# Moving one output store in the last batch and casting W1 in eighths in the first, in a fused attention and MLP kernel

## The chip, the cores and the metric

The kernel runs on one core of a Trainium2 chip. The metric is the time of one execution in microseconds (us) on the device. Profiles give times from the first instruction of the program; the span of a profile is some 1.8 us shorter than the time of the same execution.

## The reference, cut to what matters

```python
# u, v: 8 x 3008 x 256, z: 8 x 3008 x 64, all float32
scores = (1 / S) * z @ z.transpose(0, 2, 1)
out = u * ((np.maximum(scores, 0) ** 2) @ v)          # per batch
x = out.reshape(24064, 256)
h = x @ w_in                                          # 256 x 2048
g = h / (1 + np.exp(-1.702 * h))
return g @ w_out                                      # 2048 x 256
```

## The kernel before

The eight batches follow one another. A batch has six query chunks of 512 rows (`i` = 0 to 5; "the fourth chunk" is `i` = 3). Each chunk runs through attention steps `n` (its slots); at fixed slots other work is put in: scores for a later chunk (`take`), loads, turns. The last chunk or the one before it is also interleaved with the up projection, in groups of 256 hidden columns (`up_group`); the down projection follows. Scores are symmetric, so blocks of the attention matrix are reused, transposed by DMA (`tt`, `ad`, `al`, all issued by SyncE, in order).

```python
def cast_w(k):                 # ScalarE: a float32 quarter of W1 to float16
    act.activation(W1[:, :, k * DFF // 4:(k + 1) * DFF // 4], WS.pop(k), AF.Copy, scale=1.0)
...
CASTW = {(3, 8): 0, (3, 40): 1, (4, 8): 2, (4, 14): 3}     # (chunk, slot): quarter, first batch only
...
elif name == "P3" and k > NCH - 3 and b < B - 1:
    LAST2.append(lambda: store(b, k))      # the last two blocks of a batch are stored in the next batch
...
if i == 3 and n in (3, 26) and LAST2:      # where they are stored
    LAST2.pop(0)()
...
if b == 0 and i == NCH - 1 and n in (8, 30, 42):
    wsums.pop(0)()                         # VectorE: sums of blocks of W2; the first needs W2's quarters 1 and 2
```

`store` makes a transposing copy on VectorE and issues four DMAs from SyncE.

Of the kernel before, what the change touches and what calls it, by code (L numbers as in the profile page):

```python
# [15 lines left out]
def kernel(  # L16
# [13 lines left out]
    AF = mybir.ActivationFunctionType  # L30
# [4 lines left out]
    DFF = moe_w_in.shape[1]  # L35
# [20 lines left out]
    dve, act, pe, sp, pool = nc.vector, nc.scalar, nc.tensor, nc.sync, nc.gpsimd  # L56

    const = ctx.enter_context(tc.tile_pool(name="const", bufs=1))
    W1 = const.tile([P, NCC, DFF], F16, name="W1")
# [17 lines left out]
    ZP, WS = {}, {}  # L77
# [43 lines left out]
    def first_cast(g, by_act=False):  # L121
        m = g % CB * CB
        for c in range(2):
            dst, src = ZT["st"][g // CB][:, m:m + CB, c, :], ZT["f"][g // CB][:, m:m + CB, :]
            if by_act:
                act.activation(dst, src, AF.Copy, scale=1.0)
            else:
                dve.tensor_copy(dst, src)

    def first_zt(g):  # L130

        z2 = ZT["st"][g // CB][:, g % CB * CB:(g % CB + 1) * CB]
        zp = ZP[g] if g in ZP else ps1.tile([P, CB, P], F16, name="zp", tag="ps1")
        for k in range(CB):
            pe.transpose(zp[:, k, :], z2[:, k, :, :], ident)  # L135

        def copies():
            zt = ZT[0][:, g * CB:(g + 1) * CB, :].rearrange("d n p -> d (n p)")
            nb = CB if g < NCH - 1 else CB - 1
            dst = zt[:, :nb * P].rearrange("d (p n) -> d p n", n=nb)  # L140
            src = zp[:, :nb, :].rearrange("d n p -> d p n")
            if g in (0, 2, 3):
                act.activation(dst, src, AF.Copy, scale=1.0)  # L143
            else:
                dve.tensor_copy(dst, src)
            if nb < CB:
                dve.tensor_copy(zt[:, nb * P:], zp[:, nb, :])

        return copies


    def load_z(b):
        ZT[b] = pz.tile([P, NJ, P], F16, name="ZT", tag="ZT")
        for n0 in range(0, NJ, NU):
            zst = pw.tile([P, NU, 2, DQK], F16, name="zst", tag="y")
            full = min(NU, NJ - 1 - n0)
            src = z[b, n0 * P:(n0 + full) * P].rearrange("(n p) d -> p n d", p=P)
            pool.dma_start(zst[:, :full, 0, :], src)
            if full < NU:
                for h in range(2):  # L160
                    pool.dma_start(zst[h * SREM:(h + 1) * SREM, full, 0, :], z[b, S0:S])
            pool.tensor_copy(zst[:, :, 1, :], zst[:, :, 0, :])
            sp.dma_start_transpose(ZT[b][:, n0:n0 + NU], zst.rearrange("p n c d -> p (n c d)"))
# [24 lines left out]
    def load_u(b, i):  # L188
        eng = pool if b else sp
        n = width(i)  # L190
        uq = pu.tile([P, CH // QW, QW, NCC], F32, name="uq", tag="uq")
        src = u[b, i * CH:i * CH + n].rearrange("(q t) c -> t q c", t=QW)
        for k in range(P // QW):
            cs = slice(k * NCC * QW, (k + 1) * NCC * QW)
            eng.dma_start(uq[k * QW:(k + 1) * QW, :n // QW].rearrange("t q c k -> t q (c k)"), src[:, :, cs])  # L195
        UQ[b, i] = uq

    def turn_u(b, i):
        n = width(i)
        ut = pu.tile([P, NCC, CH // QW, QW], F32, name="ut", tag="ut")  # L200
        UT[b, i] = ut
        dve.transpose(
            ut[:, :, :n // QW, :].rearrange("p k q t -> p q k t"),
            UQ.pop((b, i))[:, :n // QW].rearrange("p q c k -> p q k c"),
        )
# [114 lines left out]
    def full(b):  # L320

        return NCH - 2 if b < B - 1 else NCH - 1
# [116 lines left out]
    def load_w(k):  # L439

        if k < 2:
            hold = const.tile([P, 1], F16, name=f"hold{k}")
            pool.tensor_copy(hold, XT[0, k + 1][:, 0, :1])
        if k < 4:
            WS[k] = pw.tile([P, NCC, DFF // 4], F32, name="wst", tag="y")
            pool.dma_start(WS[k], moe_w_in.rearrange("(p k) f -> p k f", k=NCC)[:, :, k * DFF // 4:(k + 1) * DFF // 4])
        else:
            fs = slice((k - 4) * CB, (k - 3) * CB)
            pool.dma_start(W2[:, fs], moe_w_out.rearrange("(fo p) c -> p fo c", p=P)[:, fs])

    def cast_w(k):
        act.activation(W1[:, :, k * DFF // 4:(k + 1) * DFF // 4], WS.pop(k), AF.Copy, scale=1.0)  # L452

    def weight_sums():
        b11, b12, b21, b22 = W2K[:, LO, 0], W2K[:, LO, 1], W2K[:, HI, 0], W2K[:, HI, 1]
# [108 lines left out]
    LAST2 = []  # L564
# [67 lines left out]
    LOADW = {  # L632
        (2, 16): 0, (3, 0): 1, (3, 9): 2, (3, 41): 3, (4, 28): 4, (4, 34): 5, (4, 40): 6, (5, 0): 7,
    }
    CASTW = {(3, 8): 0, (3, 40): 1, (4, 8): 2, (4, 14): 3}
    LOAD = {(3, NJ + 20): 4, (4, NJ + 5): 5}

    FIRST_ZT, FIRST_CAST = {12: 4, 20: 5}, {5: 4, 13: 5}
# [11 lines left out]
    def take(b, n):  # L650
        for post_ in scores(b, [queue.pop(0) for _ in range(n)]):
            post_()

    def fill(b):
        assert not queue
        queue.extend(u_ for i in range(NCH) for u_ in pieces(b, i))
# [28 lines left out]
    for b in range(B):  # L685
        nup = NCH * NFG
        more = b + 1 < B
        sched = SCHED0 if b == 0 else SCHED if more else SCHED_LAST
        turn, load = (TURN, LOAD) if b else (TURN0, LOAD0)
        head = 0  # L690
        for i in range(NCH):
            host = b + 1 if more and i == NCH - 1 else b
            if host > b:
                fill(host)
                LATE.append(host)
            for n, step in enumerate(attend(b, i, b == 0 and i == 0)):
                if b == 0 and i == 0 and n in (5, 24):
                    load_u(0, n // 24)
                if b == 0 and i == 0 and n == 2:
                    copies = first_zt(3)  # L700
                if b == 0 and i == 0 and n == 3:
                    copies()
                if b == 0 and i == 0 and n in FIRST_CAST:
                    first_cast(FIRST_CAST[n], True)
                if b == 0 and i == 0 and n in FIRST_ZT:
                    first_zt(FIRST_ZT[n])()
                if (i, n) in turn:
                    turn_u(b, turn[i, n])
                if i == 3 and n in (3, 26) and LAST2:
                    LAST2.pop(0)()  # L710
                if (i, n) in load:
                    load_u(b, load[i, n])
                if b == 0 and (i, n) in CASTW:
                    cast_w(CASTW[i, n])
                if b == 0 and (i, n) in LOADW:
                    load_w(LOADW[i, n])
                if more and (i, n) == (NCH - 2, 2 if b else 16):
                    load_z(b + 1)
                if b == 0 and i == NCH - 1 and n in (8, 30, 42):
                    wsums.pop(0)()  # L720
                take(host, sched[i].get(n, 0))
                if i == full(b) and n >= HEAD and (n - HEAD) * LAGY // (2 * NJ - 10) >= head and head < LAGY:
                    up_group(b, head)
                    head += 1
                step()
        late.sort(key=lambda t: t[0])
        if more:
            for i in range(2):
                load_u(b + 1, i)
            for n0 in range(0, NJ, VB):  # L730
                load_v(b + 1, n0)
        prods = products(b)
        for q in range(head, nup):
            if more and q in (head + 14, head + 20):
                k = int(q == head + 20)
                turn_u(b + 1, k)
                load_u(b + 1, k + 2)
            up_group(b, q)
            if b == 0 and q == head + 3:
                wsums.pop(0)()  # L740
            product(b, *prods.pop(0))
            if q >= 30 and q % 2 and late:
                late.pop(0)[1]()
        steps = [lambda kp=kp: product(b, *kp) for kp in prods]
        for step in steps:
            step()
            for sum_ in [SUMS.pop(0) for _ in range(min(len(SUMS), 1 + (len(SUMS) > 4)))]:
                sum_()
            for _, turn_it in [late.pop(0) for _ in range(min(len(late), 1 + (len(steps) < 10)))]:
                turn_it()  # L750
        LATE.clear()
        if more:
            while late:
                late.pop(0)[1]()
            take(b + 1, 2)
# [30 lines left out]
```

## Time and profile before

| before | value | what it says |
|---|---|---|
| time, three runs | 1180.33, 1180.64, 1181.52 us | spread 1.2 us |
| span of the profile | 1178.3 us | |
| TensorE busy | 1171.0 us, 99% | it is the bound |
| ScalarE, VectorE busy | 72%, 74% | not the bound, but in the way at some places |

In a view of windows, each row gives the stretch, its length and, for each engine, busy time and instructions. In the chain, each piece is the start, the length and what held things up. In the timeline, a bracket at a row's end is idle time of the engine just before it, and what ended it. The lines themselves are in the prediction.

### The profile page before, as it was taken

Reading aid. Unit: us, or ns where it says so; the run is one execution under the profiler, and the core shown is the slowest. Engines: PE = TensorE matmul, PEld = TensorE weight load, DVE = VectorE, ACT = ScalarE, POOL = GpSimd, SP = SyncE. Lnnn points to the kernel's source line nnn. Section 1 sums busy time; section 2 is a strip of 40 time slices with the busy share of each in tenths; the row PEclk is TensorE's granted clock in tenths of the full one; section 3 lists DMA queues with packets and bytes.
Section 4 is the critical chain, followed back from the end, with each engine's and each line's share of the span. In section 5 each row is a group of like instructions: output and inputs, shape, how many; then the busy total and the mean of one; then the engine's idle time right before and its main releaser. Section 6 shows DMA issues by size and latency. Waiting matters only on the chain.

```text
span 1178.3 us, 23585 instructions
## 1 busy us (share of the span) xinstructions
PE 1171.0 (99%) x9284; PEld 670.0 (57%) x9284; DVE 871.0 (74%) x1455; ACT 849.4 (72%) x1033; POOL 209.4 (18%) x294
## 2 busy tenths in 40 slices
PE   9999999999999999999999999999999999999998
PEld 3546764466644675446754467544674456744566
DVE  7789875878767786587865878658786587764776
ACT  7888874688647886478864787647877578772785
POOL 3033101231012310143101420024100241001000
PEclk9999999999999999999999999999999999999999
DMA  9998679766798677976779568895678955696023
GB/s 223 210 134 129 130 119 158 90 108 135 119 150 94 108 141 127 144 101 93 146 117 154 101 93 149 137 150 88 100 126 142 142 105 94 122 166 120 1 37 73
DMA packets 459039, 143.65 MB, mean 122 GB/s; under 512 B 424624, under 2 KB 453040, under 8 KB 458928
## 3 DMA queue, kind: packets, MB, share of 16 engines
q1 hardware_dynamic: 402464, 102.36, 52.8%
q0 software_dynamic: 55104, 38.49, 21.5%
q8 instruction: 72, 1.18, 0.4%
q10 hardware_dynamic: 1360, 1.31, 0.4%
q14 instruction: 39, 0.32, 0.1%
HBM read 60.29 MB, written 24.64 MB: 72 GB/s over the span
## 4 chain that ended last, share of the span: by engine, by line
PE 98%; ACT 1%; DMA 0%; issue 0%; SPq 0%; DVE 0%
PE o L367 40%; PE hg L408 28%; PE st L532 23%; PE sc L235 6%; PE st L535 1%; PE yp L506 1%; ACT rl L256 0%; DMA tt<-a 0%; PE w L99 0%; ACT W L452 0%; SPq L599 0%; ACT ZT L143 0%; ACT gf L416 0%; PE zp L135 0%; DVE a L270 0%
## 5 line engine op out<-in xcount | busy, mean ns | idle before, releaser
L416 ACT ACTIVATE gf<-hg 128x1024 f32<-128x1024 f32 (+1 forms) x384 | 385.3, 1004 | 114.6 <-PE hg L408 97.7
L256 ACT ACTIVATE rl<-sc 128x1024 f16<-128x1024 f32 (+1 forms) x301 | 287.4, 993 | 143.5 <-PE sc L235 98.4
L367 PEld LDWEIGHTS <-V 64*128 64x128 f16 (+1 forms) x4098 | 219.7, 94 | 252.5 <-issue 9.4
L408 PE MATMUL hg<-xt,W 128*128 128x512 f16 (+1 forms) x1408 | 354.6, 374 | 0.2
L367 PE MATMUL o<-a,V 64*128 64x512 f16 (+3 forms) x2278 | 296.1, 368 | 0.3 <-DVE a L270 0.3
L420 DVE TENSOR_SCALAR gt<-gf 128x1024 f16<-128x1024 f32 (+1 forms) x288 | 200.1, 695 | 114.2 <-ACT gf L416 113.1
L270 DVE TENSOR_TENSOR a<-rl 128x1024 f16<-128x1024 f16 (+1 forms) x266 | 178.1, 674 | 110.4 <-ACT rl L256 109.6
L195 POOL DMA_DIRECT2D uq<-in_u_dram x168 | 111.7, 673 | 739.9 <-PE sc L235 537.1
L367 PE MATMUL o<-tt,V 64*128 64x512 f16 (+1 forms) x1518 | 232.5, 377 | 1.0 <-DMA tt<-a 0.9
L408 PEld LDWEIGHTS <-W 128*128 128x128 f16 x1536 | 149.4, 98 | 125.6 <-issue 2.6
L532 PEld LDWEIGHTS <-WT 128*128 128x128 f16 x1472 | 139.1, 98 | 45.1
L532 PEld LDWEIGHTS <-W 128*128 128x128 f16 x1104 | 104.7, 98 | 32.2
L235 PE MATMUL sc<-ZT 64*128 64x512 f16 (+3 forms) x688 | 115.5, 356 | 0.6 <-ACT ZT L143 0.3
L418 ACT ACTIVATE gt<-gf 128x1024 f16<-128x1024 f32 (+1 forms) x96 | 98.9, 1030 | 3.1
L549 ACT ACTIVATE y<-st 128x256 f32<-128x256 f32 x192 | 70.6, 368 | 35.6 <-PE st L532 29.0
L532 PE MATMUL st<-gt,WT 128*128 128x256 f16 (+1 forms) x736 | 91.9, 268 | 0.0
L532 PE MATMUL st<-s,WT 128*128 128x256 f16 (+1 forms) x736 | 90.8, 268 | 0.0
L532 PE MATMUL st<-gt,W 128*128 128x256 f16 (+1 forms) x736 | 90.8, 268 | 0.0
L553 DVE SCALAR_TENSOR_TENSOR y<-st,y 128x256 f32<-128x256 f32 (+1 forms) x144 | 57.7, 408 | 24.5 <-ACT y L549 11.5
L384 DVE TENSOR_TENSOR xt<-o,ut 128x512 f16<-128x512 f32 x80 | 51.4, 683 | 28.5 <-PE o L367 28.5
L486 DVE TENSOR_TENSOR s<-s,gt 128x1024 f16<-128x1024 f16 (+1 forms) x96 | 65.0, 678 | 1.1
L484 DVE TENSOR_TENSOR s<-gt 128x1024 f16<-128x1024 f16 (+1 forms) x96 | 65.4, 681 | 0.0
(59 smaller groups left out, 670.9 us busy)
## 6 DMA issues: line engine op xcount, KB each, us to landing
out_dram<-yo SPq DMA_DIRECT2D x156, 128.0 KB, 2.8
uq<-in_u_dram POOLq DMA_DIRECT2D x140, 128.0 KB, 3.3
V<-in_v_dram POOLq DMA_DIRECT2D x35, 256.0 KB, 6.1
tt<-a SPq DMA_TRANSPOSE x232, 3.5
uq<-in_u_dram POOLq DMA_DIRECT2D x28, 112.0 KB, 4.7
out_dram<-yo SPq DMA_DIRECT2D x28, 96.0 KB, 6.4
uq<-in_u_dram SPq DMA_DIRECT2D x20, 128.0 KB, 4.3
wst<-in_moe_w_in_dram POOLq DMA_DIRECT2D x4, 512.0 KB, 6.0
```

The costliest lines, as they stand in the source:

```text
L195: eng.dma_start(uq[k * QW:(k + 1) * QW, :n // QW].rearrange("t q c k -> t q (c k)"), src[:, :, cs])
L235: pe.matmul(sc[:, r, :q1 - q0], zt[h, 2 * kp + r, :], zt[h].rearrange("d n p -> d (n p)")[:, q0:q1], start=True, stop=True,)
L256: act.activation(rl[:, :, :n], sc[:, :, :n], AF.Relu, scale=csc)
L270: dve.tensor_tensor(a[:, :, :n], rl[:, :, :n], rl[:, :, :n], ALU.mult)
L367: ins = pe.matmul(acc[c][:, :n], V16[b][h, j].rearrange("p (c k) -> p k c", k=NCC)[:, c], weights(b, i, j)[h], start=(k, m) == first[c], s ...
L408: pe.matmul(hg[:, e, :n], W1[:, c, ff * P:(ff + 1) * P], XT[b, i][:, c, :n], start=(c == 0), stop=(c == NCC - 1),)
L416: act.activation(gf[:, :, :n], hg[:, :, :n], AF.Gelu_apprx_sigmoid, scale=1.0 / FSC)
L418: act.activation(g, gf[:, :, :n], AF.Copy, scale=FSC)
L420: dve.tensor_scalar(g, gf[:, :, :n], FSC, None, ALU.mult)
L484: dve.tensor_tensor(s_, a21, a22, ALU.add)
L532: pe.matmul(bank, right[:, ff], lhs()[:, f], start=first, stop=last, skip_group_check=True)
L549: act.activation(y[:, c, :, o], bank, AF.Copy, scale=1.0 / FSC)
```

## The change

It has two independent parts. The second deferred store of the last batch moves from slot 26 of the fourth chunk to slot 14 of the fifth, so that a transpose doesn't have to queue behind it. The four casts of W1 become eight of half the size, in the fifth chunk spread out between the gelus, so that no up group waits for a whole quarter.

```diff
     def cast_w(k):
-        act.activation(W1[:, :, k * DFF // 4:(k + 1) * DFF // 4], WS.pop(k), AF.Copy, scale=1.0)
+        h = slice(k % 2 * DFF // 8, (k % 2 + 1) * DFF // 8)
+        act.activation(W1[:, :, k // 2 * DFF // 4:][:, :, h], WS[k // 2][:, :, h], AF.Copy, scale=1.0)
+        if k % 2:
+            del WS[k // 2]
...
-    CASTW = {(3, 8): 0, (3, 40): 1, (4, 8): 2, (4, 14): 3}
+    CASTW = {(3, 7): 0, (3, 8): 1, (3, 40): 2, (3, 41): 3, (4, 5): 4, (4, 8): 5, (4, 12): 6, (4, 14): 7}
...
-                if i == 3 and n in (3, 26) and LAST2:
+                if (i, n) in ((3, 3), (3, 26) if more else (4, 14)) and LAST2:
```

## The prediction

> **What bounds the kernel now.** I read the page of the kernel before first (busy shares, the chain that ended last), then the busy time by windows, then the chain and the timeline in the two places that the windows pick out.
>
> ```profile
> PE 1171.0 (99%) x9284; PEld 670.0 (57%) x9284; DVE 871.0 (74%) x1455; ACT 849.4 (72%) x1033; POOL 209.4 (18%) x294
> ...
> PE 98%; ACT 1%; DMA 0%; issue 0%; SPq 0%; DVE 0%
> ```
>
> TensorE is busy for 1171.0 of 1178.3 us and carries 98% of the chain. Nothing in the change takes a matmul away or makes one shorter, so it can only close some of the 1178.3 - 1171.0 = 7.3 us in which TensorE had nothing to run. The busy time by windows says where those are (columns: length, then busy time of each engine).
>
> ```profile
> 0.00:25.00 25.00, 22.98 (x128) 8.90 (x130) 17.61 (x31) 18.64 (x24) 10.45 (x18) 1.00 1.07 239
> 25.00:62.00 37.00, 36.96 (x342) 18.94 (x339) 27.67 (x43) 33.04 (x37) 3.09 (x6) 1.00 1.11 201
> 62.00:75.00 13.00, 12.76 (x59) 5.49 (x58) 8.26 (x13) 11.72 (x14) 2.96 (x4) 1.00 1.17 146
> 75.00:1075.00 1000.00, 1000.00 (x7979) 574.31 (x7978) 746.23 (x1253) 716.96 (x876) 190.38 (x264) 1.00 0.78 124
> 1075.00:1082.00 7.00, 6.03 (x56) 2.47 (x54) 2.05 (x4) 1.27 (x2) 0.00 (x0) 1.00 0.93 139
> 1082.00:1178.30 96.30, 92.31 (x732) 59.92 (x728) 69.14 (x113) 67.73 (x85) 2.50 (x4) 0.99 0.18 38
> ```
>
> In the thousand microseconds in the middle TensorE is never idle. The start (about 2 us) and the tail (about 4 us) are not touched. The change works in the two short windows: 62 to 75 us, where ScalarE casts W1 between the gelus of the first up-projection groups, and 1075 to 1082 us, in the last batch.
>
> The last batch first. The chain of waits between 1072 and 1084 us (start, length, what):
>
> ```profile
> 1073.18 0.63 DVE a L270
> 1073.80 0.14 DVE a L273
> 1073.95 0.07 SPq L599
> ...
> 1075.24 0.47 SPq L599
> 1075.71 0.06 issue
> 1075.76 0.02 SPq L298
> 1075.78 0.05 issue
> 1075.83 4.57 DMA tt<-a
> 1080.39 0.04 issue
> 1080.44 1.04 PE o L367 x8
> ```
>
> The attention block `a` is squared by 1073.94. Its transposing DMA (L298) stands behind four stores (L599) in the queue of SyncE, is issued only at 1075.83 and lands at 1080.39; TensorE goes on at 1080.44. In the timeline the four matmuls before that wait start at 1078.90 and are issued as two row-tiled pairs at 0.216 us each, so TensorE was free again at 1078.90 + 0.43 = 1079.33: **1.11 us lost**.
>
> Then the first batch, from its timeline:
>
> ```profile
> 66.99 1.05 ACT L452 ACTIVATE W<-wst 128x1024 f16<-128x1024 f32 x1
> ...
> 67.38 0.59 PE L367 MATMUL o<-tt,V 128*128 128x512 f16 x2
> 67.94 1.01 ACT L416 ACTIVATE gf<-hg 128x1024 f32<-128x1024 f32 x1
> 68.09 0.55 PEld L408 LDWEIGHTS <-W 128*128 128x128 f16 x4 [0.61 <-ACT W L452]
> ```
>
> The fifth up group needs the third quarter of W1, whose cast ends at 68.04. TensorE's two matmuls started at 67.38, so it was free at 67.38 + 2 x 0.216 = 67.81 and started at 68.09: 0.28 lost. At 71.19 the same happens with the fourth quarter (three matmuls from 70.26, free at 70.91, start 71.19): 0.28. Together **0.57 us** (0.284 and 0.286 unrounded; the 0.61 of the weight load counts the prefetch that normally runs ahead of the matmuls).
>
> **What the Trainium skill says.** (1) "ScalarE: Activation LUTs", What ACT_TABLE_LOAD costs: with immediate scale and bias an ACTIVATE takes 186 ns + 0.833 ns per element, and successive ones overlap by about 93 ns. For 1024 elements that is 1039 ns; the four casts of this trace take 1048 to 1051 ns, and the gelu after the cast of 66.99 starts 0.95 us later: it agrees. (2) "Perfetto Trace Analysis", Optimizing Scalar/DVE Operations: where Scalar isn't saturated but causes bubbles on others, "breaking up instructions may allow work to be completed sooner". That is the intent here; no run has shown it yet. (3) The same page, DMA Instruction — HWDGE: the sequencer is held until the descriptors are generated, and the movement lies outside the bar. It agrees: the transpose is issued in 1.25 us and lands 4.57 us after its start, and it couldn't start while the stores were being issued. (4) "DMA: Bandwidth & Descriptors", Issuing engines are not separate DMA queues: DMAs of all engines interleave on the same 16 engines. In the window the transposes take 3.2 to 4.7 us (median 4.4) to land, the long ones being those that run beside stores and u loads.
>
> **Part A, the store.** The second deferred store of the seventh batch's output (one 0.97 us transposing copy on VectorE at 1071.81 and the four stores, 1073.24 to 1075.71) leaves slot 26 of the fourth chunk. By the order of the instructions, SyncE now has the two transposes of `tt` directly after one another, then the two of `al`, and only then the four stores. So:
> - The second `tt` transpose can be issued at about 1074.0, just after its square, not at 1075.83: 1.85 us earlier.
> - Time to landing: 3.2 us at the least, as those around 1060, up to 4.6 us beside the u loads that are in flight until about 1076.7. It lands between 1077.2 and 1078.6.
> - TensorE wants the tile at 1079.33, its weight load some 0.2 us before. The wait is gone with 0.5 us or more to spare: **-1.11 us**.
> - What moves: VectorE makes the copy after the square that ends at 1077.37; its next work is at 1082.17, so it is hidden. SyncE issues the stores from about 1080.5 (the `al` transposes begin at 1077.44 as before and end at 1080.4) for 2.5 us. They meet the u loads that POOL issues from 1082.27; those land by 1086.89 and are first read at 1092.45, so even 2 us more cost nothing. **0**.
>
> **Part B, the casts.** Each quarter of 1024 elements becomes two of 512. By the formula of the skill an eighth takes 613 ns and holds ScalarE for 613 - 93 = 520 ns; a quarter holds it 946 ns (0.95 in the trace). Two eighths cost 1.04 for 0.95: 0.09 us more per quarter, 0.38 us in all.
> - In the chunk before (quarters 1 and 2, the eighths still side by side) ScalarE runs without a gap from 50.30 to 55.60, and TensorE lost 0.16 and 0.13 us there to scores that waited for a free PSUM pair. I take the extra of the first cast as passed on in full: **+0.09 us**. The second cast (60.24) has no score close behind that waits; its 0.09 only moves the first gelu from 63.79 to 63.88.
> - In the chunk of the first up groups I ran ScalarE's new order by hand (gelu 0.91 from start to start, eighth 0.52; gelus and eighths numbered as the groups, from 1): gelu1 63.88, eighth5 64.79, gelu2 65.31, gelu3 66.22, eighth6 67.13, gelu4 67.65, eighth7 68.56, gelu5 69.08, eighth8 69.99, gelu6 70.51. TensorE would reach group 5 at 67.81 (its eighth is done by 65.4), group 6 at 69.10 (done 67.8), group 7 at 70.61 (done 69.2), group 8 at 71.90 (done 70.6): no cast is waited for, and each group's PSUM pair (gelu two groups before, ended 1.02 after its start) is free in time. The tightest is group 4, which wants 66.52 against gelu2's end at 66.33. **-0.57 us**.
> - The load of the last quarter landed at about 68.2 (issued 61.59, 6.6 to landing); eighth7 starts at 68.56, close but after it.
>
> **Sum:** -1.11 - 0.57 + 0.09 = -1.59 us, from 1180.64 to 1179.05, which I round to 1179.0. Since TensorE is never idle in the middle, what is won at 70 us should arrive at the end in full.
>
> **The rivals.** First: *the transposes stay late*, because what delays them is the traffic rather than the place in the queue. For it: the first `tt` transpose, not behind any store, still took 4.7 us. Against: the store's share of that traffic leaves too, and even 4.6 us is in time. If it holds, up to 0.5 us of the 1.11 remains: about 1179.5. Second: *ScalarE becomes the bound between 64 and 72 us*, since gelu2 now stands behind a cast. For it: ScalarE is busy 11.72 of 13 us in that window and gets 0.2 us more, and the margin of group 4 is 0.19 us. Against: TensorE had waited for ScalarE there only at the casts. If an eighth cost 0.65 in place of 0.52, some 0.1 to 0.3 us would return: 1179.3. Third: *the moved store hurts where it goes*, delaying the `al` transposes or the last u loads. The order of SyncE's queue speaks against it; it would give back up to 1 us: about 1180. Fourth: nothing arrives because something after 75 us runs on its own clock, a DMA with no slack; the full 1000.00 of 1000.00 speaks against it. That would be 1179.5, part A alone.
>
> **Range and chances.** The three runs before spread over 1.2 us (1180.33 to 1181.52), as much as the gain, so the median alone may be off by 0.4 us. With that on the rivals' figures I take 1178.2 to 1180.0. 2% is 23.6 us; all idle time of TensorE is 7.3 us, so faster by over 2% is impossible by this change, and nothing in it could cost 23 us: 0.99 for the same.
>
> **What would show it.** Right: in the profile after, no wait of TensorE for `tt` near 1079 us; the second `tt` transpose issued at about 1073.5 (that place then comes 0.5 us earlier) directly after the first; the stores after `al`; no weight load waiting for the cast; casts of about 0.61 us; span about 1176.7. Wrong: a wait for `tt` of over 0.2 us, a new wait of TensorE for a gelu or a cast between 62 and 75 us, more than 0.2 us lost between 50 and 58 us, or a span longer than 1177.8.

## The result, and the profile after

| | before | changed |
|---|---|---|
| median of six runs | 1180.49 us | 1179.57 us |
| lowest, highest | 1180.13, 1183.37 | 1178.64, 1180.72 |
| span of the profiled run | 1178.3 | 1178.5 |

The ratio is 0.9988 with a 95% interval of 0.9975 to 1.0001. Here and below ratios and intervals are of the same rounds; they are not quite the ratios of the medians, or of the means, of the times that are quoted. The median lies in the stated range, 0.6 us above the predicted figure. The six times are the odd thing: 1178.64, 1178.69 and 1178.92, then 1180.21, 1180.32 and 1180.72. The profiled execution took 1180.32, so it is of the upper three, and its span, 1178.5, is no shorter than before's; it lies above the 1177.8 that the prediction named as a sign of being wrong.

The page of the changed kernel, engines and chain:

```profile
PE 1171.9 (99%) x9284; PEld 670.2 (57%) x9284; DVE 870.5 (74%) x1455; ACT 849.6 (72%) x1037; POOL 208.0 (18%) x294
...
PE 96%; ACT 1%; DMA 1%; issue 1%; POOL 0%; DVE 0%; DVEq 0%; POOLq 0%; ACTq 0%
```

DMA and GpSimd have appeared in the chain. The windows of before, asked again:

```profile
62.00:75.00 13.00, 13.00 (x61) 5.78 (x60) 8.26 (x14) 12.14 (x16) 1.95 (x3) 1.00 1.21 148
75.00:1075.00 1000.00, 999.31 (x7966) 573.98 (x7966) 745.01 (x1250) 717.06 (x876) 189.92 (x265) 1.00 0.78 123
1075.00:1082.00 7.00, 6.97 (x68) 3.04 (x66) 3.16 (x7) 1.09 (x2) 0.00 (x0) 1.00 0.79 117
```

Both windows that the change aims at are full now: 13.00 of 13.00 (12.76 before) and 6.97 of 7.00 (6.03 before). But the thousand microseconds between them, full before, have a hole.

**The store.** SyncE's queue in the timeline, and then the chain around it:

```profile
1073.20 3.28 SPq L298 DMA_TRANSPOSE tt<-a  x2
1078.72 2.70 SPq L277 DMA_TRANSPOSE al<-a  x2
1081.54 2.09 SPq L602 DMA_DIRECT2D out_dram<-yo  x4
```

```profile
1073.47 3.24 PE o L367 x30
1076.71 0.19 PE sc L235 x2
1076.90 4.75 PE o L367 x44
1081.65 0.08 PE sc L235 x2
```

The two transposes of `tt` stand together, `al` follows, and the stores come last. The second one is issued at 1075.25, right after its square, and lands at 1079.32. Where the chain before ran through the stores and 4.57 us of DMA, TensorE now runs 44 matmuls without a break.

**The casts.** ScalarE and the weight loads in the timeline of the first batch:

```profile
67.47 0.64 ACT L453 ACTIVATE W<-wst 128x512 f16<-128x512 f32 x1
...
67.98 0.74 PEld L408 LDWEIGHTS <-W 128*128 128x128 f16 x4
...
69.39 0.63 ACT L453 ACTIVATE W<-wst 128x512 f16<-128x512 f32 x1 [0.36 <-DMA wst<-in_moe_w_in_dram]
...
70.78 0.75 PEld L408 LDWEIGHTS <-W 128*128 128x128 f16 x4
```

No weight load waits for a cast. One cast itself waited 0.36 us, for the load of the last quarter of W1, which had landed only at about 69.4.

**What took the gain back.** The chain between 77 and 98 us:

```profile
77.53 5.34 DMA zst<-in_z_dram
...
83.02 1.04 POOL zst L162
84.05 0.72 POOL W L449
84.78 7.31 DMA W<-in_moe_w_out_dram
...
92.18 0.10 DVE WT L461
...
95.70 0.93 ACT rl L256
96.63 0.04 issue
96.67 0.39 PE sc L235 x2
```

VectorE, before (first line) and after (second), at the first sum of W2 blocks:

```profile
90.33 1.22 DVE L458 TENSOR_TENSOR WT<-W 128x1024 f16<-128x1024 f16 x1
```

```profile
92.18 1.23 DVE L461 TENSOR_TENSOR WT<-W 128x1024 f16<-128x1024 f16 x1 [1.78 <-DMA W<-in_moe_w_out_dram]
```

That sum (L458 before, L461 now) needs the second quarter of W2. In the profile before, VectorE's sequencer saw it landed at 89.8 (a view of one line gives count, duration in ns, first and last start), and VectorE came to the sum at 90.33: half a microsecond of slack that no wait shows.

```profile
L458 DVEq EVENT_SEMAPHORE  x1: 21/21/21, 89.8 to 89.8; - x1
```

After the change the landing came at 92.1, and VectorE stood still for 1.78 us in a stretch where, before, it was busy for 16.00 of 16 us (84 to 100). The squares of the scores behind it came late, and two scores of TensorE waited. From the score matmuls at the head of that chunk to the next up group, the timeline has 86.80 to 97.40 before, 10.60 us, and 86.71 to 98.39 after, 11.68: 1.08 us lost.

Why W2 came so late can be read from issues and landings in the two traces. This load was issued 1.21 us later (84.78 against 83.57), mostly because the first load of the second batch's z, ahead of it in GpSimd's queue, took 6.33 us to land in place of 5.00; and it took 7.31 us itself in place of 6.19. The 5.00 us of the profile before is the shortest of all fourteen profiles (twelve have 5.08 to 6.72, one 10.11), so the slack that it showed was in part luck. The change also has a share: measured from the first up group, the new casts, whose end frees the buffer for that load of z, let it be issued 0.30 us earlier, but TensorE goes on 0.46 us earlier here, and 0.59 us earlier where no cast is late.

### The profile page after: what moved, and what is told of

Read it like the earlier page. It is cut to its first block, busy times and chain, and to the rows that moved or that the text cites. A ratio compares the mean times of both kernels' runs of the same rounds, so it can differ in the third digit from the quotient of the medians.

```text
span 1178.5 us, 23592 instructions
## 1 busy us (share of the span) xinstructions
PE 1171.9 (99%) x9284; PEld 670.2 (57%) x9284; DVE 870.5 (74%) x1455; ACT 849.6 (72%) x1037; POOL 208.0 (18%) x294
## 4 chain that ended last, share of the span: by engine, by line
PE 96%; ACT 1%; DMA 1%; issue 1%; POOL 0%; DVE 0%; DVEq 0%; POOLq 0%; ACTq 0%
PE o L367 39%; PE hg L408 26%; PE st L535 23%; PE sc L235 6%; PE st L538 1%; DMA W<-in_moe_w_out_dram 1%; PE yp L509 1%; ACT rl L256 1%; DMA zst<-in_z_dram 0%; PE w L99 0%; ACT gf L416 0%; POOL zst L162 0%; POOL zst L158 0%; ACT W L453 0%; ACT L416 0%
```

## The experiments

The question was why the times fall into groups, and whether the terms of the prediction hold once that is set aside. Twelve kernels ran, four on a chip at a time and in five rounds each, so each has five or six times. All results were correct. The kernel before ran beside them: 11, 11 and 9 times.

**Groups of times or noise.** The changed kernel again (no edit).

> The changed kernel itself, once more. Theory W (the first weight sum of VectorE waits for the second quarter of W2, in some executions, and takes back what the change wins): two groups of times, near 1178.7 and near 1180.4 us, and the profile shows whichever group it fell in, with the wait of the weight sum (1.8 us in the first profile) in the slow group alone. Rival N (plain noise): times spread evenly over 1178.5 to 1180.8, with no tie to that wait.

Measured: 1178.67, 1179.35, 1179.69, 1179.77, 1181.24 and 1181.61 us, ratio 0.9986 (0.9973 to 0.9999). Not two clean groups, and the wait is not in the slow ones alone as expected: the profiled execution, with 1179.77 one of the middle ones, has it again, 2.6 us on VectorE, longer than in the first profile, and TensorE idle for 1.08 us in the window 80 to 110. The kernel before spread as widely beside it: 1180.02 to 1180.40 four times, then 1181.15 to 1182.48 six times, and 1185.16. So high times are not the change's own.

**Each part alone.**

```diff
 e2_store_only: the kernel before with
-                if i == 3 and n in (3, 26) and LAST2:
+                if (i, n) in ((3, 3), (3, 26) if more else (4, 14)) and LAST2:
 e3_casts_only: the changed kernel with that line as before
```

> Only the moved store of the last batch. By the prediction 1.11 us under before: about 1179.2 where before is 1180.3, and no wait of TensorE for the transposed tile near 1079 us. Theory W with the casts as its trigger: no slow group here beyond what before shows. Rival (the wait for W2 is there whatever the casts do): a slow group some 1.6 us above the fast one here as well.

> Only the casts in eighths. By the prediction 0.57 - 0.09 = 0.48 us under before in executions without the wait for W2: about 1179.8, with the wait for the tile near 1079 us still there (about 1.1 us). Theory W with the casts as its trigger: a slow group about 1.6 us above, near 1181.4, in about half of the executions.

The store alone: 1178.70 to 1181.54, median 1179.28, ratio 0.9984 (0.9969 to 0.9998). Its chain runs through 44 unbroken matmuls at 1075.49; the weight loads wait for the cast 1.2 us in all, as before. It has VectorE waiting 1.0 us for W2, with the old casts, and TensorE lost nothing by it. The casts alone: 1179.73 to 1182.04, median 1181.01, ratio 0.9994 (0.9982 to 1.0006). The lowest one is the profiled one; it has no wait for W2, no weight load waiting for a cast, and the old wait for `tt`:

```profile
1075.42 4.54 DMA tt<-a
1079.96 0.05 issue
1080.01 1.04 PE o L367 x8
```

Its span is 1177.9, which is 0.4 under before's 1178.3, where 0.48 was expected. That closeness is partly chance: by the count of matmuls further below, 0.22 of it was there before the first cast, the casts won 0.46, and some 0.25 was lost elsewhere. Still, each part does its own work, and the wait for W2 comes with either kind of casts.

**Splitting or spacing.**

```diff
 e5_side_by_side: the changed kernel with
-(4, 5): 4, (4, 8): 5, (4, 12): 6, (4, 14): 7
+(4, 8): 4, (4, 9): 5, (4, 13): 6, (4, 14): 7
```

> The changed kernel with the eighths of quarters three and four side by side where the quarters stood (slots 8 and 9, 13 and 14) in place of spread out. If the splitting is what helps (TensorE need only wait for the first half of a quarter): no wait of TensorE for a cast over 0.1 us, times as the changed kernel's in both groups. If the spacing is what helps: 0.28 us lost at each of the two places again, 0.5 us slower than the changed kernel.

Measured: 1178.32 to 1180.36, median 1178.69, ratio 0.9981 (0.9969 to 0.9993). The weight loads wait for a cast 0.4 us in all, which is part of the prefetch; in the chain groups 2 to 9 begin 63.96 to 73.50, 9.54 us apart, against 10.08 (63.87 to 73.95) in the kernel before and 9.50 (64.28 to 73.78) in the run with late sums below, whose casts are the changed kernel's. Nearly all of the gain is in the splitting; the slots are worth 0.04 us in these profiles. VectorE waits for W2 here too, 1.0 us, at no cost to TensorE.

**The wait for W2, taken away and brought nearer.**

```diff
 e4_sum_late: the changed kernel, e7_before_sum_late: the kernel before, with
-                if b == 0 and i == NCH - 1 and n in (8, 30, 42):
+                if b == 0 and i == NCH - 1 and n in (28, 36, 42):
 e6_before_sum_early: the kernel before, with n in (2, 30, 42)
```

> The changed kernel with the first two weight sums placed at slots 28 and 36 of the sixth chunk in place of 8 and 30, so that they come some 3 us later and W2 has landed. Theory W: one group of times only, near 1178.7 us, no wait of VectorE for W2 and no TensorE loss near 95 us. Rival N: the same spread as the changed kernel.

> The kernel before with the first weight sum at slot 2 in place of 8, about 1 us earlier. In its profile W2 had landed 0.57 us ahead of that sum. Theory W (the sum stands near the landing of W2 in the kernel before too): VectorE waits for W2 some 0.4 us or more, and times rise by up to 1 us, to 1180.3 to 1182. Rival (only the new casts make that wait): no wait, 1180.3.

> The kernel before with the first two weight sums at slots 28 and 36. Theory W: its typical time stays at 1180.3 us, and executions as the two high ones of before (1181.5, 1183.4) are gone, if they were of the same kind. Rival: high ones remain.

The changed kernel with late sums: 1178.37, 1178.39, 1178.54, 1178.67, 1178.88 and 1179.03, median 1178.61, ratio 0.9974 (0.9962 to 0.9985). All six lie below 1179.1, where the changed kernel in the same rounds reached 1181.61. VectorE doesn't wait for W2, and TensorE is busy for 30.00 of the 30 us from 80 to 110 (29.33 in the changed kernel's first profile).

With the sum earlier, the kernel before takes 1182.23 to 1188.53, ratio 1.0031 (1.0013 to 1.0048): even its lowest is over 2 us above before's lowest there (1179.94). Its waits between 84 and 100 us (who waited for whom, total, times, longest):

```profile
DVE WT L458 <- DMA W<-in_moe_w_out_dram: 1.9, 1, 1.9
PE sc L235 <- ACT rl L256: 1.8, 1, 1.8
```

The wait for W2 thus needs none of the new casts; and the cost was larger than the 1 us that I expected. In this profile W2 also landed later (90.89 against 89.76), so the earlier sum, by about 1.2 us, is not the whole of it. The profile is of the 1182.62 execution; what made the times above 1184 is not shown.

The kernel before with late sums missed the expectation: 1179.78, 1180.45, 1180.46, 1181.13 and 1182.62, ratio 0.9997 (0.9985 to 1.0009). The wait for W2 is gone from its profile, but that execution, the 1182.62 one, met another:

```profile
61.69 1.25 DVE L202 STREAM_TRANSPOSE ut<-uq 128x1024 f32<-128x1024 f32 x1 [2.94 <-DMA uq<-in_u_dram]
```

The u load of block 3 was issued some 2.6 us later than in the profile before (51.70 against 49.04), behind transposes in SyncE's queue, and landed late. VectorE waited 2.94 us for it, and TensorE lost 1.68 by the count of matmuls.

**Whole quarters in the fourth chunk, eighths in the fifth.**

```diff
 e8_best: e4_sum_late with
     def cast_w(k):
+        if k < 4:
+            if k % 2 == 0:
+                act.activation(
+                    W1[:, :, k // 2 * DFF // 4:(k // 2 + 1) * DFF // 4], WS.pop(k // 2), AF.Copy, scale=1.0)
+            return
```

> The moved store, the late weight sums, and eighths in the fifth chunk only, the first two quarters cast whole as before. By the working of the prediction 0.09 us better than the changed kernel with late sums: about 1178.6 us in one group, 1.7 us under before.

Measured: 1178.19 to 1180.66, median 1179.91, ratio 0.9986 (0.9974 to 0.9998): no better, and not one group. The profiled execution (1180.66) again has VectorE waiting for u, 2.64 us, for a load issued as late (51.91).

**Both chance waits taken away.** The last four kernels have the late sums and this edit:

```diff
-    LOAD0 = {(1, 14): 2, (2, 12): 3, (2, NJ + 20): 4, (4, 8): 5}
+    LOAD0 = {(1, 14): 2, (2, 2): 3, (2, NJ + 20): 4, (4, 8): 5}
```

> The kernel before with both chance waits of the first batch taken away: the first two weight sums at slots 28 and 36, and the u load of block 3 at slot 2 of the third chunk in place of 12 (two transposes earlier in SyncE's queue). If the two waits make the spread: one tight group near 1180.2 us (the low group of before) and no wait of VectorE for W2 or u. If something else makes it: times from 1180 to 1183 as before.

> The same two edits, with the moved store: 1.11 us under the clean kernel before by the prediction, 1.1 to 1.3 by the profiles so far (lost there 1.65 to 1.87 us before, 0.55 after): about 1179.0.

> The same two edits, with the whole change: 1.59 us under the clean kernel before by the prediction; by the profiles so far -1.1 to -1.3 for the store, -0.58 for the two waits for casts, +0.13 for the eighths in the fourth chunk, about 1.65 in all: about 1178.6, tight.

> The same two edits with the store and with eighths in the fifth chunk only, whole quarters in the fourth. By the sum 0.1 us better than the clean changed kernel, about 1178.5, and tight, where the same kernel without the early u load ran from 1178.2 to 1180.7. If that kernel's wait for u had another cause than SyncE's queue, high times remain.

| run | base | lowest to highest | median | ratio, interval |
|---|---|---|---|---|
| e9_clean_before | before | 1180.29 to 1183.14 | 1181.44 | 1.0002, 0.9989 to 1.0015 |
| e10_clean_store | store only | 1179.12 to 1186.59 | 1179.59 | 0.9985, 0.9971 to 0.9999 |
| e11_clean_after | changed | 1178.21 to 1179.15 | 1178.69 | 0.998, 0.9967 to 0.9992 |
| e12_clean_best | e8_best | 1178.16 to 1181.71 | 1179.03 | 0.9984, 0.9971 to 0.9998 |

The changed kernel is tight at the expected place, and its five times don't differ from those of e4_sum_late. The three others are not tight, so the two waits are not all. Two of the profiles show a third one, of the cast for the load of the last quarter of W1; first e12, then the 1186.59 execution of e10 (ScalarE in both):

```profile
69.68 0.63 ACT L458 ACTIVATE W<-wst 128x512 f16<-128x512 f32 x1 [1.17 <-DMA wst<-in_moe_w_in_dram]
```

```profile
74.92 1.06 ACT L452 ACTIVATE W<-wst 128x1024 f16<-128x1024 f32 x1 [4.12 <-DMA wst<-in_moe_w_in_dram]
```

In e10 that load took 12.70 us in the chain (62.19 to 74.89), and TensorE, idle for 4.35 us, then ran at a granted clock of 0.54 from 76 to 82; by the count of matmuls it lost 6.95 us. The Trainium skill has this: "TensorE: Matmul & The Clock Gate", What's actually happening, says that an idle window of about 3.4 us puts the array back to half clock, until it has been busy for about as long; the trace agrees as to the fall (to 0.50 at 74.7, 3.1 us after the last matmul), and here the clock came back only at about 81.6, 5.5 us after the matmuls had gone on.

## Why the prediction was right or wrong

The time was inside the range and the forecast of no change beyond 2% held. Point by point:

- **The store, -1.11 us: right.** In every profile with the moved store TensorE waits for no `tt` tile near 1079 us, and in every one without it it does. The rival that the traffic keeps the transposes late fell: issued in time, the second one landed within 3.4 to 4.1 us.
- **The two waits for casts, -0.57: right, and for the reason given.** Groups 2 to 9 begin 10.08 us apart before and 9.50 with the changed casts: -0.58. The changed kernel's own first profile lost 0.1 of it to the late load of the last quarter, the margin that the prediction called "close". The rival that ScalarE becomes the bound fell.
- **The eighths in the fourth chunk, +0.09: right for the first cast, 0.04 short for the second.** From the score matmuls at 48.99 to those at 59.20 the chain has 10.21 us before. The same stretch, 49.40 to 59.70, has 10.30 in e11, 49.24 to 59.45 has 10.21 in e9 with whole quarters. The second cast, taken as free, cost another 0.04 us before the first up group. An eighth took 619 to 658 ns against the 613 of the formula.
- **"What is won at 70 us should arrive at the end in full": the step that failed.** It rested on one profile, in which TensorE is busy for 1000.00 of 1000.00. A full window says that nothing waited in that execution; it doesn't say how much room there was. The fourth rival (something after 75 us on its own clock, a DMA with no slack) was dismissed on that ground, and it is what the profiled execution shows: the first sum of W2 blocks had 0.5 us of slack before and waited 1.78 us here. Even more than that rival allowed came back: 1.08 us lost against the 0.5 won by the casts.

As to size, whole times mix the change with these waits. A cleaner count, made afterwards from the traces, goes by matmuls: each trace holds all 9284 matmuls of TensorE, in the same order, so the n-th matmul can be set against the n-th of the profile before. The table says how far it came later (+) or earlier (-) in each stretch (us, rounded).

| | until 49 us | casts, fourth chunk | casts, fifth chunk | wait for W2 | store | rest | sum |
|---|---|---|---|---|---|---|---|
| predicted | 0 | +0.09 | -0.57 | 0 | -1.11 | 0 | -1.59 |
| changed, first profile | +0.25 | +0.13 | -0.46 | +1.06 | -1.12 | +0.31 | +0.17 |
| changed again, e1 | -0.27 | +0.13 | -0.59 | +1.47 | -1.12 | 0.00 | -0.38 |
| changed, late sums, e4 | +0.28 | +0.13 | -0.59 | 0.00 | -1.12 | +0.02 | -1.27 |
| e11 | +0.41 | +0.13 | -0.59 | 0.00 | -1.12 | +0.12 | -1.04 |

The store wins 1.12 us in all nine profiles that have it moved. So the two wins were sized to 0.02 us, and without the wait for W2 they arrive nearly in full: the terms of the change sum to -1.58, and from 49 us on e4 gained 1.54 and e11 1.45. The 0.31 in the rest of the first profile was lost near 220 and 515 us, where no wait of TensorE shows; its cause stays open.

The first column is a source of spread that the experiments did not look at. Before the first cast the fourteen executions already lie 1.07 us apart (-0.27 to +0.80). In the latest, e8, VectorE waits 1.46 us for one of the very first loads of z, a wait that the profile before doesn't have:

```profile
7.40 0.49 DVE L128 CAST zst<-zf 128x256 f16<-128x256 f32 x2 [1.46 <-DMA zf<-in_z_dram]
```

Moving the sum later takes the wait for W2 away, and the changed kernel's six times then lie within 0.7 us at 1178.6; moving it earlier makes the wait in the kernel before. All eleven times of the changed kernel with late sums (e4 and e11) are at most 1179.15 us; eight of its own twelve lie above 1179.3. That the wait took the gain back in the two profiled executions is therefore shown, 1.06 and 1.47 us. That it makes the whole difference of the medians (1179.73 against 1178.61 in the same rounds) is not: the intervals of the two ratios overlap a little.

The predicted median was met with some luck, since neither this loss nor the start was in the sum. The mean of the changed kernel's twelve times is 1179.82, that of the 17 times of the kernel before in the same rounds 1181.41: 1.59 us, the forecast itself, but the high times of both kernels are in it and such close agreement is partly chance.

What stays open: how often each of the late loads comes. Of the six profiles of kernels with the sum at its old slot, four have the wait for W2 (1.0, 1.0, 1.8 and 2.6 us; the two of 1.0 cost TensorE nothing), with old and with new casts. Waits for u, and waits of over 0.4 us for the last quarter of W1, were seen only in kernels that cast the first two quarters whole (five of eight profiles, none of six with eighths in both chunks). An effect of the casts in the fourth chunk isn't shown by that: in e7 and e8, which have the two long waits for u, that load was already issued over 2 us late before the first of those casts began (51.70 against 51.85 us, 51.91 against 52.02), and these are the two executions that had started latest (+0.63 and +0.80). Nor did any profile catch the unmodified kernel before in one of its high times, so their cause is only presumed to be of this kind.

The best version is the changed kernel with the sums at slots 28 and 36: 1178.61 us against 1179.73 for the changed kernel and 1181.51 for the kernel before in the same rounds, still well inside 2%.

## What to carry to other kernels

When one engine is busy all the time, what is left to win is found by listing its few idle stretches, and a cost worked out from the chain there can be right to 0.1 us. Before counting on such a gain, look also for loads that land just ahead of their first use: a view of waits shows none of them until an execution in which one lands late, so take several profiles, and move the use, not only the load. When the order of an engine's instructions doesn't change, setting the n-th of one trace against the n-th of another tells what each stretch won or lost, which whole times and busy shares don't. A small consumer in the middle of a saturated in-order queue, here one sum of 1.2 us on VectorE, passes a late load on to everything behind it.

## What the Trainium skill lacked or had wrong

- "DMA: Bandwidth & Descriptors" gives bandwidths, fixed costs and a latency under load, but in what I read of it not how much one transfer's landing varies between executions of nearly the same program when the engines are saturated. The last quarter of W1 (512 KB) took 8.15 us to land in e12 and 12.70 in e10, with a median of 5.7 to 6.5 us for the four quarters in each profile; the first load of z for the second batch took 5.00 to 6.72 us in thirteen profiles and 10.11 in e10.
- "Perfetto Trace Analysis", Optimizing Scalar/DVE Operations, advises breaking up instructions that cause bubbles. That held (10.08 to 9.54 us with the halves still side by side); it doesn't say that spreading the halves out adds next to nothing (a further 0.04).
- No page that I read says that a wait of zero in a profile tells nothing about slack. Here 0.5 us of it was gone in other executions, where the same instruction waited 1.0, 1.78 and 2.6 us.
